# A longer hand-written order at the start of a convolution, Fourier and MLP kernel: the first MLP step's hidden layer and the rest of that step go inside it, and W2 is converted ahead of the third step's statistics

## The chip, the core and the metric

The kernel runs on one core of one Trainium2 chip. The metric is the device time of one execution in microseconds. The engines are TensorE (PE; PEld are its weight loads), VectorE (DVE), ScalarE (ACT), GpSimd (POOL) and SyncE (SP), which issues most of the DMAs.

## What is computed

The reference, cut to what matters. B, S and D are 8, 4224 and 192, the hidden layer has 768 columns.

```python
def _attn_ref(x, weight):                      # 8 heads of 24 columns, 7 taps
    w = softmax(weight)                        # written out with exp and sums
    x_pad = concatenate([zeros((B, 6, D)), x], axis=1)
    ...
    return einsum('hk,bskhg->bshg', w, x_unf)  # a causal convolution over the sequence

def _moe_ref(x, w_ch1, w_ch2):
    mixed = real(fft(fft(x, axis=1), axis=2))
    u = x + mixed
    un = (u - mean(u)) / sqrt(var(u) + 1e-06)  # over the 192 columns
    return u + maximum(un @ w_ch1, 0.0) @ w_ch2
```

The MLP's input is the convolution's output.

## The kernel before

The work is cut into 8 batches (`first` is batch 0, `second` is batch 1) and each batch into 9 steps of the MLP (512 tokens each in steps 0 to 7, 128 in the last). Tile names end in batch and step: `hh_0_1` belongs to step 1 of batch 0. The profile leaves these numbers out.

A batch runs through these stages:

- Convolution, six chunks (`conv_unit`, three parts each): TensorE multiplies windows `xt` with a band matrix into `pc`, ACT copies that to `xa`, DMA stores it to a scratch tensor `sc` in DRAM. ACT also squares `xt` (`sq`), for a scale per batch (`scales`: a norm matmul `pn_x`, a root, `s_x`).
- Split: DMA loads `xs` from `sc` in four pieces (`load_x`), ACT writes the scaled high half in 16 bits to `XH`, DVE the remainder to `XL` (`split_x`, two halves for each piece).
- Fourier stages: `stage_a` (16 tiles, `pa` to `yh` on ACT and `yl` on DVE), `stage_b` (8 tiles, `pb` to `V` on ACT and its low part on DVE, then a small POOL copy to `V0`), and a last product `pq` in `prep`.
- Preparation of a step (`prep`): `pq` to `u` (ACT and POOL; for steps 0 and 1 of batch 0, called `early`, on DVE), the residual rows `xr`, fetched by POOL with four indirect DMAs a step (`load_res`), the statistics (`st`, `mv` on DVE, a root `sd` on ACT, small POOL operations up to `nm`), the normalised `un`, its 16-bit high part `hl` (ACT) and the remainder of `hl` (a subtraction on POOL), then a DMA transpose `kt` on SP (`transposes`).
- MLP of a step: `mlp_hidden`, six groups of five matmuls `ph` (1 group for 128 hidden columns), each read by ACT (`hh`) and DVE (`hlo`); `mlp_out`, 72 matmuls `po` with `W2` and a DVE addition to `u`, then the store.

W1 and W2 come as float64 and are converted on DVE with integer operations (`from_float64`, ten of them for each piece, `cv` and `raw` in the names), scaled by a power of two from their norm (`square_w`, `pow2_of_norm`) and split into high and low parts.

Each engine takes its instructions in one order. Up to the end of the start (all of batch 0's front part, convolution of batch 1, the preparation of steps 0 and 1, the W2 scale) that order is the order in which the code is written: the class `InOrder` puts each instruction behind the last of its engine. Behind `nc.release()` a scheduler orders all that follows. The loop over 72 steps begins there, with `n` = 0: for each it lists the MLP's units and spreads over them the preparation of the steps ahead and the front of the later batches. PSUM tiles named `f` (four buffers) hold `pc`, `pa`, `pb`, `pq` and `pn_x` in turn, those named `h` (two) hold `ph`, those named `o` (two) `po`.

## Time and profile before

| | |
|---|---|
| median of 3 runs | 1275.69 us (1275.05 to 1276.0) |
| the profiled execution, own time | 1266.83 us |
| its span | 1265.0 us |
| mean granted TensorE clock | 0.973 |
| busy in the span: PE, PEld | 1177.6 us (93%), 937.0 us (74%) |
| busy: DVE, ACT, POOL | 753.8 us (60%), 825.7 us (65%), 658.1 us (52%) |

The profiled execution is one execution with the profiler on. Its times run from the first instruction, and sums are made against its span. TensorE is busy for 93% of the span as a mean over the program; the start is different from the rest, so the stretches have to be read apart. In rows of single instructions the columns are the start and the duration in us, engine, line, operation and tiles; what stands in brackets is the idle time of the engine ahead of it and what ended it. The line is 137 for nearly all, since `InOrder` issues them.

### The profile page before, as it was taken

Reading aid. Unit: us, or ns where it says so; the run is one execution under the profiler, and the core shown is the slowest. Engines: PE = TensorE matmul, PEld = TensorE weight load, DVE = VectorE, ACT = ScalarE, POOL = GpSimd, SP = SyncE. Lnnn points to the kernel's source line nnn. Section 1 sums busy time; section 2 is a strip of 40 time slices with the busy share of each in tenths; the row PEclk is TensorE's granted clock in tenths of the full one; section 3 lists DMA queues with packets and bytes.
Section 4 is the critical chain, followed back from the end, with each engine's and each line's share of the span. In section 5 each row is a group of like instructions: output and inputs, shape, how many; then the busy total and the mean of one; then the engine's idle time right before and its main releaser. Section 6 shows DMA issues by size and latency. Waiting matters only on the chain.

```text
span 1265.0 us, 30104 instructions
## 1 busy us (share of the span) xinstructions
PE 1177.6 (93%) x12224; PEld 937.0 (74%) x12224; DVE 753.8 (60%) x1638; ACT 825.7 (65%) x1575; POOL 658.1 (52%) x1036
## 2 busy tenths in 40 slices
PE   4087889999999999998999999999999989999999
PEld 4086668786877878786877878787777867777767
DVE  5685575466556665655665666565755756455444
ACT  4476786587667876568666886577665765555642
POOL 0136553457455655556545673566645575557420
PEclk9597999999999999999999999999999999999999
DMA  8956694686425853386534774358462433224321
GB/s 287 260 128 154 155 230 128 161 196 169 114 70 158 215 136 93 101 187 174 145 95 130 188 175 109 84 148 190 109 135 77 110 91 72 76 64 85 75 60 45
DMA packets 225899, 170.19 MB, mean 135 GB/s; under 512 B 119576, under 2 KB 207456, under 8 KB 225760
## 3 DMA queue, kind: packets, MB, share of 16 engines
q1 hardware_dynamic: 175160, 117.86, 38.9%
q0 software_dynamic: 12672, 25.97, 7.1%
q10 hardware_dynamic: 37928, 24.44, 7.1%
q8 instruction: 95, 1.56, 0.5%
q14 instruction: 44, 0.36, 0.1%
HBM read 83.73 MB, written 58.55 MB: 112 GB/s over the span
## 4 chain that ended last, share of the span: by engine, by line
PE 68%; DMA 7%; DVE 7%; POOL 7%; ACT 5%; issue 4%; SPq 0%; ACTq 0%; DVEq 0%; POOLq 0%
PE ph L137 27%; PE po L137 23%; PE pa L137 6%; PE pq L137 4%; PE pc L137 4%; PE pb L137 4%; POOL xr L137 4%; DVE XL L137 3%; DMA kt<-hl 3%; DMA xs<-sc 2%; ACT un L137 1%; ACT XH L137 1%; POOL u L137 1%; ACT hh L137 1%; POOL hl L137 1%
## 5 line engine op out<-in xcount | busy, mean ns | idle before, releaser
L137 PE MATMUL ph<-kt,W 128*128 128x512 f16 (+1 forms) x2160 | 498.1, 364 | 11.7 <-DMA kt<-hl 6.6
L137 DVE SCALAR_TENSOR_TENSOR hlo<-ph,hh 128x512 f16<-128x512 f32 (+1 forms) x400 | 271.9, 681 | 332.7 <-ACT hh L137 331.8
L137 PE MATMUL po<-W,hh 128*128 128x192 f16 x3168 | 428.7, 247 | 11.4 <-ACT hh L137 8.7
L137 ACT ACTIVATE hh<-ph 128x512 f16<-128x512 f32 (+1 forms) x400 | 237.0, 593 | 303.4 <-PE ph L137 294.2
L137 PE MATMUL po<-W,hlo 128*128 128x192 f16 x1584 | 388.7, 247 | 0.6 <-DVE hlo L137 0.6
L137 POOL DMA_INDIRECT xr<-sc,rows_sb x264 | 291.3, 1103 | 133.7 <-issue 59.9
L137 PEld LDWEIGHTS <-hh 128*128 128x128 f16 x3168 | 282.9, 98 | 45.1 <-ACT hh L137 10.5
L137 PEld LDWEIGHTS <-W 128*128 128x128 f16 x2160 | 193.9, 98 | 153.5 <-issue 17.6
L137 POOL TENSOR_TENSOR u<-u,xr 128x768 f32<-128x768 f32 (+1 forms) x70 | 119.1, 1702 | 123.1 <-ACT u L137 122.9
L137 POOL TENSOR_TENSOR hl<-un,hl 128x512 f16<-128x512 f32 (+1 forms) x144 | 128.4, 914 | 90.7 <-ACT hl L137 90.1
L137 PEld LDWEIGHTS <-hlo 128*128 128x128 f16 x1584 | 155.5, 98 | 16.5 <-DVE hlo L137 0.9
L137 ACT ACTIVATE un<-u,nm,y 128x192 f32<-128x192 f32 x256 | 120.0, 541 | 18.4 <-POOL nm L137 18.4
L137 PE MATMUL pc<-xt,band 128*120 128x144 f32 x756 | 114.1, 295 | 17.9 <-DMA band<-line_d 13.2
L137 PE MATMUL pa<-c_sb,XH 128*128 128x128 f16 x1024 | 104.2, 221 | 23.9 <-ACT XH L137 23.9
L137 PEld LDWEIGHTS pc<-xt,band 128*120 128x120 f32 x756 | 105.1, 190 | 27.1 <-issue 13.2
L137 DVE SCALAR_TENSOR_TENSOR yl<-pa,yh 99x512 f16<-99x512 f32 x128 | 86.6, 688 | 60.7 <-ACT yh L137 60.0
L137 DVE SCALAR_TENSOR_TENSOR XL<-xs,s_x,XH 128x768 f16<-128x768 f32 x64 | 111.0, 1741 | 15.2 <-ACT XH L137 15.0
L137 ACT ACTIVATE XH<-xs,s_x 128x768 f16<-128x768 f32 x64 | 106.2, 1677 | 10.7 <-DMA xs<-sc 10.7
L137 PEld LDWEIGHTS <-XH 128*128 128x128 f16 x1024 | 82.6, 98 | 35.2 <-ACT XH L137 24.0
L137 DVE SCALAR_TENSOR_TENSOR u<-po,fo,u 128x384 f32<-128x384 f32 (+1 forms) x136 | 80.9, 595 | 43.7 <-PE po L137 42.5
L137 PE MATMUL pb<-c_sb,yh 99*128 99x102 f16 (+1 forms) x1040 | 93.4, 210 | 7.3 <-DVE V L137 5.9
L137 PE MATMUL pq<-c_sb,V 128*128 128x130 f16 (+1 forms) x1440 | 99.2, 218 | 0.0
(126 smaller groups left out, 1264.6 us busy)
## 6 DMA issues: line engine op xcount, KB each, us to landing
out_dram<-u SPq DMA_DIRECT2D x64, 384.0 KB, 2.6
xt<-in_xw_dram SPq DMA_DIRECT2D x42, 576.0 KB, 5.2
xs<-sc SPq DMA_DIRECT2D x96, 192.0 KB, 4.0
sc<-xa ACTq DMA_DIRECT2D x30, 540.0 KB, 6.1
xs<-sc SPq DMA_DIRECT2D x32, 216.0 KB, 3.8
sc<-xa SPq DMA_DIRECT2D x12, 540.0 KB, 5.7
xr<-sc,rows_sb POOLq DMA_INDIRECT x264
xt<-in_xv_dram SPq DMA_DIRECT2D x6, 504.0 KB, 4.7
```

What stands on the lines that cost most here:

```text
L137: made = op(*a, **k)
```

## The change

`InOrder` and `Engines` are gone. All instructions built so far are chained, engine by engine, by one call of `keep_order` at the end of the hand-written part, and the loop begins with `n` = 1. What the loop did for step 0 is now written out by hand, in another order:

- The six hidden units of step 0 (`hid[0]` to `hid[5]`) stand among the convolutions of batch 1 and the conversion of W2, ahead of W2's scale.
- W2's scale, its split and the output scale stand ahead of the statistics of step 2 (`stats`).
- The subtraction for `hl` in steps 0 and 1 goes from POOL to DVE.
- The gathers of the residual rows for steps 2 and 3 are issued earlier.
- Chunks 4 and 5 of batch 1's convolution, and its scale, come later; the loads `xs_1_0` and `xs_1_1` come behind the transpose of step 2. Chunk 4's windows take a buffer of `xs` instead of `hh`.
- The rest of step 2's preparation, `u` of step 3 and `stage_b` up to tile 6 are in the written part too.

```diff
+def keep_order(tc):
+    info = mybir.DependencyInfo(
+        mybir.DependencyClass.NoSync, mybir.DependencyReason.DATA
+    )
+    last = {}
+    for ins in tc.nc.cur_bb.bb.instructions:
+        if ins.engine in last:
+            tc.add_manual_dep(ins, last[ins.engine], info, reason="keep_order")
+        last[ins.engine] = ins.name
...
-            nc.gpsimd.tensor_tensor(
+            engine = nc.vector if early else nc.gpsimd
+            engine.tensor_tensor(
                 bl[:, :, o : o + n], un[:, :ng, f], hi[:, :, f], op=ALU.subtract
...
-                load_windows(second, ch, *(("hlo", 2), ("hh", 2), ("hh", 2))[ch - 3])
+                load_windows(second, ch, *(("hlo", 2), ("xs", 2), ("hh", 2))[ch - 3])
...
+    hid = [call(mlp_hidden, first, 0, hts) for hts in hidden_units(0)]
     stage_b(first, 0)
     stage_b(first, 1)
+    for f in gathers(2):
+        f()
     prep_piece(0)
...
     for part in range(2):
         conv_unit(second, 3, part)
     prep_piece(1)
-    for f in gathers(3):
-        f()
+    hid[0]()
     conv_unit(second, 3, 2)
     transposes(first, 1)
     some(half, 2)
+    hid[1]()
     stage_b(first, 2)
-    chunk(second, 4)
     some(half, 2)
+    hid[2]()
+    some(half, 2)
+    hid[3]()
+    some(half, 3)
     total, *stats = sums(2)
     total()
-    some(half, 2)
-    chunk(second, 5)
-    stage_b(first, 3)
-    some(half, 3)
+    hid[4]()
     square_w("w2", mlp["w2_1"], 1)
-    for f in stats:
-        f()
-    stage_b(first, 4)
-    mlp["s2"] = last(pow2_of_norm(mlp["nw2"], 2, 15, "w2"))
+    norm = pow2_of_norm(mlp["nw2"], 2, 15, "w2")
+    next(norm)
+    hid[5]()
+    next(norm)
+    chunk(second, 4)
+    mlp["s2"] = last(norm)
     for i in range(2):
         split2(i)
     output_scale()
-    nc.release()
-    for n in range(len(steps) + 1):
+    for f in stats:
+        f()
+    stage_b(first, 3)
+    for f in gathers(4):
+        f()
+    scale, normal, parts = rest(2)
+    scale()
+    chunk(second, 5)
+    normal()
+    stage_b(first, 4)
+    parts()
+    transposes(first, 2)
+    total, *stats = sums(3)
+    total()
+    last(scales(second))
+    for i in range(2):
+        load_x(second, i)
+        load_windows(batches[2], i)
+    stage_b(first, 5)
+    for f in stats:
+        f()
+    stage_b(first, 6)
+    keep_order(tc)
+    for n in range(1, len(steps) + 1):
```

`keep_order` only fixes the sequence among the instructions of the written part. The scheduler may still put instructions of the loop between them, and does. Below, numbers behind batch and step only tell the tiles of the program apart.

On DVE, around the end of W2's conversion (`raw_w2_1`), before; the statistics of step 2 (`st_0_2`) are the next work, and W2's scale follows behind `V` of tiles 4 and 5:

```order
L137 TENSOR_TENSOR cv0_w2_1_857<-cv0_w2_1_857,raw_w2_1_351 128x576
L137 TENSOR_SCALAR cv1_w2_1_858<-raw_w2_1_351 128x576
L137 SCALAR_TENSOR_TENSOR raw_w2_1_351<-cv1_w2_1_858,cv0_w2_1_857 128x576
L137 BN_STATS st_0_2_1041<-u_0_2_960 128x6
L137 BN_AGGR mv_0_2_1042<-st_0_2_1041 128x2
L137 BN_STATS st_0_2_1041<-u_0_2_960 128x6
L137 BN_AGGR mv_0_2_1042<-st_0_2_1041 128x2
```

And now:

```order
L271 SCALAR_TENSOR_TENSOR raw_w2_1_351<-cv1_w2_1_863,cv0_w2_1_862 128x576
L770 SCALAR_TENSOR_TENSOR hlo_0_0_897<-ph_0_0_4_1004,hh_0_0_896 128x512
L220 TENSOR_REDUCE tot_w2_1014<-nrm_w2_359 128x1
L770 SCALAR_TENSOR_TENSOR hlo_0_0_897<-ph_0_0_5_1018,hh_0_0_896 128x512
L226 TENSOR_SCALAR r_w2_1026<-pn_w2_1016 128x1
L229 RECIPROCAL r_w2_1026<-r_w2_1026 128x1
L231 TENSOR_SCALAR s_w2_1048<-r_w2_1026 128x1
L234 TENSOR_SCALAR s_w2_1048<-s_w2_1048 128x1
L357 SCALAR_TENSOR_TENSOR W2_77<-w2f_265,s_w2_1048,W2_77 128x3x192
L357 SCALAR_TENSOR_TENSOR W2_77<-raw_w2_1_351,s_w2_1048,W2_77 128x3x192
L365 TENSOR_TENSOR fo_78<-s_w1_335,s_w2_1048 128x1
L366 RECIPROCAL fo_78<-fo_78 128x1
```

The scale `s_w2`, both low parts of `W2` and the output scale `fo` now come directly behind the conversion, with the last two `hlo` of step 0 between; `st_0_2` is the next row.

On POOL, the subtractions for `hl` and the gathers `xr` ahead of step 2's `u`, before:

```order
L137 TENSOR_TENSOR hl_0_0_801<-un_0_0_785,hl_0_0_801 128x4x128
L137 TENSOR_TENSOR hl_0_0_801<-un_0_0_785,hl_0_0_801 128x4x64
L137 DMA xr_0_2_805<-sc_0_147,rows_sb_83 128x192 x4
L137 TENSOR_TENSOR hl_0_1_887<-un_0_1_871,hl_0_1_887 128x4x128
L137 TENSOR_TENSOR hl_0_1_887<-un_0_1_871,hl_0_1_887 128x4x64
L137 DMA xr_0_3_891<-sc_0_147,rows_sb_83 128x192 x4
L137 DMA xr_0_4_1164<-sc_0_147,rows_sb_83 128x192 x4
L137 COPY V0_0_658<-V_0_2_907 128x12x8
L137 TENSOR_TENSOR u_0_2_960<-u_0_2_960,xr_0_2_805 128x768
```

And now, the rows from step 2's `u` up to `nm_0_2`, which `un_0_2` on ACT needs:

```order
L659 TENSOR_TENSOR u_0_2_981<-u_0_2_981,xr_0_2_692 128x768
L580 COPY V0_0_658<-V_0_3_1067 128x12x8
L593 DMA xr_0_4_1099<-sc_0_147,rows_sb_83 128x192 x4
L689 TENSOR_SCALAR w_0_2_1107<-mv_0_2_1058 128x4
L690 TENSOR_SCALAR nm_0_2_1108<-mv_0_2_1058 128x4
L692 TENSOR_TENSOR t_0_2_1106<-y_0_2_1105 128x4
L593 DMA xr_0_5_1381<-sc_0_147,rows_sb_83 128x192 x4
L693 TENSOR_TENSOR t_0_2_1106<-t_0_2_1106,w_0_2_1107 128x4
L694 TENSOR_SCALAR t_0_2_1106<-t_0_2_1106 128x4
L695 TENSOR_TENSOR y_0_2_1105<-y_0_2_1105,t_0_2_1106 128x4
L696 TENSOR_TENSOR nm_0_2_1108<-nm_0_2_1108,y_0_2_1105 128x4
```

The subtractions of steps 0 and 1 have left POOL. The gathers `xr_0_2` and `xr_0_3` stand further up, behind `V0` of tiles 0 and 1; `xr_0_4` now stands behind the copy of `V_0_3`, and `xr_0_5` (from the loop) between the operations that lead to `nm_0_2`.

On SP, the transposes `kt` and the loads `xs` of batch 1, before:

```order
L137 DMA xs_1_0_1266<-sc_1_715 32x9x192 x2
L137 DMA_TRANSPOSE kt_0_2_1283<-hl_0_2_1279 128x12x128
L137 DMA xs_1_1_1285<-sc_1_715 32x8x192 x4
L137 DMA xt_2_0_1300<-in_xw_dram 128x1152
L137 DMA xt_2_1_1304<-in_xw_dram 128x1152
L137 DMA xs_1_2_1383<-sc_1_715 32x8x192 x4
L137 DMA out_1_dram<-u_0_0_693 128x768
L137 DMA_TRANSPOSE kt_0_3_1544<-hl_0_3_1489 128x12x128
L137 DMA xs_1_3_1420<-sc_1_715 32x8x192 x4
```

And now:

```order
L804 DMA out_1_dram<-u_0_0_698 128x768
L732 DMA_TRANSPOSE kt_0_2_1178<-hl_0_2_1174 128x12x128
L501 DMA xs_1_0_1218<-sc_1_720 32x9x192 x4
L375 DMA xt_2_0_1223<-in_xw_dram 128x1152
L501 DMA xs_1_1_1225<-sc_1_720 32x8x192 x4
L375 DMA xt_2_1_1230<-in_xw_dram 128x1152
L804 DMA out_1_dram<-u_0_1_742 128x768
L501 DMA xs_1_2_1383<-sc_1_720 32x8x192 x4
L501 DMA xs_1_3_1420<-sc_1_720 32x8x192 x4
L732 DMA_TRANSPOSE kt_0_3_1544<-hl_0_3_1489 128x12x128
```

`xs_1_0` has moved behind `kt_0_2`, and `kt_0_3` behind `xs_1_3`.

More of the change, by code (lines that the diff above doesn't have):

```diff
@@ L122, in token_rows @@
     return rows
-class InOrder:
-    def __init__(self, tc, engine):
-        self.tc, self.engine, self.last, self.fixed = tc, engine, None, True
-    def __getattr__(self, name):
-        op = getattr(self.engine, name)
-        def issue(*a, **k):
-            behind = self.fixed and self.last is not None
-            with self.tc.issue_after(self.last) if behind else ExitStack():
-                made = op(*a, **k)
-            if self.fixed:
-                self.last = made.ins
-            return made
-        return issue
-class Engines:
-    def __init__(self, tc):
-        self.names = ("tensor", "vector", "scalar", "gpsimd", "sync")
-        for name in self.names:
-            setattr(self, name, InOrder(tc, getattr(tc.nc, name)))
-    def release(self):
-        for name in self.names:
-            getattr(self, name).fixed = False
+def keep_order(tc):
[7 more added lines that the diff above has]
+        last[ins.engine] = ins.name
 @with_exitstack
@@ L170 @@
 ):
-    nc = Engines(tc)
+    nc = tc.nc
     PSUM = bass.MemoryType.PSUM
@@ L862, in plan @@
         if b == 1:
-            loads = {-9: [0, 1], -8: [2, 3]}
+            loads = {-8: [2, 3]}
             splits = {-8: [0, 1], -7: [2, 3, 4, 5], -6: [6, 7]}
-            return {}, -9, loads, splits, first_a
+            return {}, None, loads, splits, first_a
         if b == 2:
@@ L883, in front @@
                 units.append(call(load_windows, bt, ch + 2))
-        if bt.b == 2 and rel == min(conv) - 1:
-            units += [call(load_windows, bt, ch) for ch in range(2)]
         if bt.b > 2 and rel in (min(conv) - 2, min(conv) - 1):
@@ L1033 @@
     prep_piece(0)
-    for f in gathers(2):
-        f()
     conv_unit(second, 1, 2)
@@ L1039 @@
     low1(2)
+    for f in gathers(3):
+        f()
     for _ in range(3):
```

2 lines of the change are left out of this document (1 added, 1 removed).

## The prediction

> **What bounds the kernel now.** I read the page first, then busy time by stretch, then TensorE's own instructions in order of time. In the windows the columns are PE, PEld, DVE, ACT and POOL busy us, the granted clock, the DMA share and GB/s.
>
> ```profile
> span 1265.0 us, 30104 instructions
> 85.50:112.70 27.20, 16.57 (x167) 15.46 (x167) 18.54 (x51) 18.32 (x39) 20.76 (x21) 0.80 0.90 217
> 112.70:180.40 67.70, 60.02 (x497) 43.66 (x496) 41.49 (x84) 51.29 (x91) 35.20 (x55) 0.93 0.71 173
> 131.50:174.80 43.30, 37.30 (x305) 27.76 (x304) 24.36 (x43) 35.60 (x57) 19.60 (x34) 0.96 0.88 210
> 180.40:300.00 119.60, 118.93 (x1297) 97.10 (x1298) 71.54 (x154) 86.70 (x165) 64.31 (x104) 1.00 0.68 164
> 300.00:1265.00 965.00, 944.30 (x9843) 744.43 (x9841) 564.94 (x1225) 622.66 (x1209) 528.57 (x845) 0.99 0.47 118
> ...
> 112.74 0.33 PE L137 MATMUL pb<-c_sb,yh 99*128 99x102 f16 x2 [5.42 <-DVE V L137]
> 115.15 2.29 PE L137 MATMUL ph<-kt,W 128*128 128x512 f16 x5
> 121.23 1.24 PE L137 MATMUL ph<-kt,W 128*128 128x512 f16 x5
> 180.42 0.23 PE L137 MATMUL pa<-c_sb,XL 128*128 128x128 f16 x1 [1.67 <-DVE XL L137]
> ```
>
> From 180.40 on TensorE is the bound: idle 0.7 of 119.6 us, then 20.7 of 965. Ahead of that it idles 10.6 us in the first stretch and 7.7 in the second. The changed rows all lie ahead of about 200 us; behind that the two orders are equal on every engine. So I look for one moment: the first `pa` matmul that reads batch 1's `XL` (180.42, after a wait of 1.67 us for DVE). The two orders put the same matmuls ahead of it, but for two of 128x128. If it comes d us later, all that follows should come d later. The question is when the last split of batch 1 ends, and whether TensorE is through with its own work by then.
>
> TensorE will be. The change puts eight `ph` groups (six of step 0, two of step 1) ahead of the first `po`, 1.24 us each, which before stood behind it; the `pb` groups of tiles 4 to 6 move the other way. Were TensorE alone the bound, most of the 18.3 idle us could go: a limit near 1262 us. But ACT and DVE must still feed the split of batch 1.
>
> **Step 1: the subtractions on DVE.**
>
> ```profile
> 85.60 0.84 ACT L137 ACTIVATE hl<-un 128x768 f16<-128x768 f32 x1 [1.46 <-DVE un L137]
> 86.53 2.50 POOL L137 TENSOR_TENSOR hl<-un,hl 128x512 f16<-128x512 f32 x2 [7.28 <-ACT hl L137]
> 86.62 1.88 DVE L137 SCALAR_TENSOR_TENSOR W<-w1a,s_w,W 128x768 f16<-128x768 f32 x1
> 95.55 1.85 POOL L137 TENSOR_TENSOR hl<-un,hl 128x512 f16<-128x512 f32 x2 [1.61 <-ACT hl L137]
> 107.57 0.76 DVE L137 SCALAR_TENSOR_TENSOR raw_w<-cv_w,cv_w 128x576 f32<-128x576 uint32 x1
> L137 DVE SCALAR_TENSOR_TENSOR hlo<-ph,hh 128x512 f16<-128x512 f32 x22 | 14.9, 683 | 20.0 <-ACT hh L137 19.9
> ```
>
> The subtraction of 768 columns has no DVE row. From the 0.76 us that a conversion takes for 576 columns with two inputs it is 1.0; the upper end is POOL's own 2.50. I take 1.0, the row of the same engine. DVE now stands still for ACT's cast (0.84 us from 85.60) and then works 1.0. Against that, `W1`'s low part took 1.88 beside POOL's subtraction; by the `hlo` row (0.68 for 512 columns) it should be 1.0 alone. Together the next step's preparation is 1.0 late on DVE, and its subtraction (1.0 in place of 1.85) ends at 97.4, as before. The first step's transpose can go 1.5 us earlier (87.5 for 89.03). POOL's gathers for steps 2 and 3 move ahead to where POOL waited 7.28 us for the cast, and cost nothing.
>
> **Step 2: W2 to the scale.** From 97.4 DVE carries, ahead of the end of the conversion, four `hlo`, two `V` and nine conversion operations.
>
> ```profile
> L137 DVE SCALAR_TENSOR_TENSOR V<-pb,V 128x408 f16<-128x408 f32 x16 | 8.8, 576 | 7.9 <-ACT V L137 7.8
> 108.42 0.72 ACT L137 ACTIVATE sq_w<-raw_w 128x576 bf16<-128x576 f32 x1 [2.63 <-DVE raw_w L137]
> 115.33 0.16 DVE L137 TENSOR_SCALAR r_w<-pn_w 128x1 f32<-128x1 f32 x1 [0.18 <-PE pn_w L137]
> 116.58 0.78 ACT L137 ACTIVATE W<-w2f,s_w 128x576 f16<-128x576 f32 x1 [0.86 <-DVE s_w L137]
> 119.52 0.15 DVE L137 RECIPROCAL fo<-fo 128x1 f32<-128x1 f32 x1
> ```
>
> Four times 0.6, two times 0.5 and about 5.6 for nine of up to 0.76 give 9.0: the conversion ends at 106.4 instead of 108.3. Then squares 0.8, norm matmul 0.8, the last `ph` of step 0, which now stands between norm and scale, 2.1 (TensorE has idled some 3.7 us for the squares, so I take the 2.29 row and not 1.24), its `hh` and `hlo` 1.1, and the scale 1.2 (115.33 to 116.58): 112.4. ACT has chunk 4's copies and a square (2.4) ahead of W2's high part; W2's two parts and `fo` take 2.5. `fo` is done at 117.3, before at 119.67: 2.4 us gained.
>
> **Step 3: the third step's statistics, POOL's queue.**
>
> ```profile
> 125.71 0.95 POOL L137 DMA_INDIRECT xr<-sc,rows_sb  x1 [0.30 <-issue]
> 131.33 0.19 POOL L137 TENSOR_TENSOR nm<-nm,y 128x4 f32<-128x4 f32 x1
> 131.55 1.87 ACT L137 ACTIVATE un<-u,nm,y 128x192 f32<-128x192 f32 x4 [0.50 <-POOL nm L137]
> L137 DVE BATCH_NORM_STATS2 st<-u 128x6 f32<-128x192 f32 x24 | 7.6, 339 | 1.9 <-POOL u L137 1.9
> ```
>
> Statistics (four, 0.34 and about 0.14 each) and `V_0_3`'s low part end at 120.2. POOL's copy of `V_0_3` waits for that, and now four gathers of 1.25 (0.95 and 0.30 of issue) stand behind that copy, then three small ones, four more gathers, then the rest: 0.3 + 5.0 + 0.8 + 5.0 + 1.1. `nm_0_2` is ready at 132.4; before 131.5. The 2.4 us are gone, on POOL.
>
> **Step 4: ACT up to the last split.** Group rows are for 76 to 182 us: busy in all, mean ns.
>
> ```profile
> L137 ACT ACTIVATE hh<-ph 128x512 f16<-128x512 f32 x22 | 13.1, 596 | 7.5 <-PE ph L137 7.4
> L137 ACT ACTIVATE xa<-pc 120x432 f32<-120x432 f32 (+1 forms) x27 | 12.3, 497 | 2.1 <-PE pc L137 1.4 <-DMA sc<-xa 0.7
> L137 ACT ACTIVATE sq<-xt 128x1152 bf16<-128x1152 f32 x10 | 11.8, 1176 | 0.0
> L137 ACT ACTIVATE V<-pb 128x408 f16<-128x408 f32 x16 | 7.6, 509 | 5.5 <-PE pb L137 5.3
> L137 ACT ACTIVATE u<-pq,g 128x384 f32<-128x384 f32 (+2 forms) x15 | 6.0, 495 | 0.4 <-PE pq L137 0.4
> 140.06 1.45 SPq L137 DMA_TRANSPOSE kt<-hl  x1
> 141.61 2.33 SPq L137 DMA_DIRECT2D xs<-sc  x4
> 145.65 1.78 POOL L137 TENSOR_TENSOR hl<-un,hl 128x512 f16<-128x512 f32 x2 [3.19 <-ACT hl L137]
> 148.52 1.61 ACT L137 ACTIVATE XH<-xs,s_x 128x768 f16<-128x768 f32 x1 [0.71 <-DMA xs<-sc]
> 173.15 1.62 ACT L137 ACTIVATE XH<-xs,s_x 128x768 f16<-128x768 f32 x1
> ```
>
> From `un_0_2` (131.55) to the last `XH` of batch 1 (174.77) ACT was busy 35.6 us and idle 7.7. The new order has in the same stretch also eight `V` (3.8) and two residual moves (2.4), and no longer four `hh` (2.4), a square (1.2) and three `xa` (1.4): 36.8. It begins at 132.4. The wait: `xs_1_0` is now loaded behind `kt_0_2`'s transpose on SP; before, it was loaded ahead of it. The transpose needs `un`, `V_0_4`, an `hh`, the cast and POOL's subtraction (1.8 + 0.9 + 0.5 + 0.8 + 1.8): 138.2, which is 1.9 earlier than before. The loads begin 1.55 later, issue for 2.33 and land 4.6 after that (143.94 to 148.52, where `XH` waited for them): 146.7. ACT's work ahead of `XH` is over at 141.2 (8.8 us after 132.4). So 5.5 us idle, and the last `XH` ends at 132.4 + 36.8 + 5.5 = 174.7. Even.
>
> **Step 5: the last `XL`.**
>
> ```profile
> 175.88 4.48 DVE L137 SCALAR_TENSOR_TENSOR XL<-xs,s_x,XH 128x768 f16<-128x768 f32 x2
> 176.42 2.65 POOL L137 TENSOR_TENSOR u<-u,xr 128x768 f32<-128x768 f32 x1 [1.53 <-ACT u L137]
> 161.28 3.43 DVE L137 SCALAR_TENSOR_TENSOR XL<-xs,s_x,XH 128x768 f16<-128x768 f32 x2
> ```
>
> On DVE `hlo_0_3_1` still stands ahead of the last two `XL`, but its `hh` now comes behind chunk 2's square: `XL` starts 1.1 later, at 177.0. The pair takes 3.43 or 4.48; POOL's addition that ran beside the slower one now follows three copies later, so it meets only the second: I take 3.9, end 180.9 against 180.36. That is d = +0.5.
> The Trainium skill (SBUF — State Buffer, "Who interferes with whom") says that a DVE operation with two inputs in SBUF and a POOL operation that reads SBUF exclude each other, and that the one issued first blocks the other. By that rule both `XL` would be through undisturbed and d near 0.0; by the 4.48 row it would be +1.1. The trace shows a slowing (4.48 for 3.43), not a full block of the pair by 2.65.
>
> **The sum.** -2.4 at `fo`, +3.3 up to `nm_0_2` on POOL, -1.0 up to the last `XH`, +1.2 up to the start of the last `XL`, -0.6 for their length: d is +0.5. The profiled execution took 1266.83 us, 1.83 more than its span; the median shown is 1275.69, 8.9 more. I carry that over: span 1265.5, median 1276.2.
>
> **Rivals.**
>
> ```profile
> DMA to landing us min/median/max: 3.7/3.9/9.2
> ```
>
> Faster: ACT's 5.5 us do not stay idle. If `xs_1_0` lands as `V_0_7` is cast, 4.7 to 5.5 us go, since the 36.8 of work bind alone: d = -4.7, 1271.0. For it speaks that TensorE is eight groups ahead; against it that the wait is on a chain of POOL, SP and DMA, which TensorE's lead does not shorten. It decides from 2.6 us of gain, that is `nm_0_2` ahead of 130.
>
> Slower: `kt_0_3`. It stands on SP behind `xs_1_3` now, and the cast for it ends 11.8 us of ACT work (two `hh`, two squares, `u`, `un`, three `xa`, two `XH`, itself) behind the first `XH` pair (146.7 and 3.4): cast 161.9, subtraction 163.7. At the usual 3.9 it lands at 167.6, its `ph` ends 168.7; `hh_0_3_0` is due on ACT at 171.2, the last `XH` pair less than 3.5 us behind it. At 9.2, the longest in the trace, the `ph` ends at 174.0 and all behind it is 2.8 late: 1279.0, and with the 7.7 us of idle that ACT had before in place of 5.5 it is 1281.2. It decides from a landing over 6.4 us. DMA was busy 0.88 of that stretch, which speaks for it.
>
> **How the numbers follow.** 0.2% of the time, 2.55 us, is about what a measurement tells from no change. My own case, d between -2.5 and +2.5, has 0.42; the faster rival 0.26; the slower 0.32, since a walk along one chain leaves out waits rather than adds them. The range reaches to both rivals, 1271.0 to 1281.5; outside lie the TensorE limit and a case with both waits and a late W2, 0.2 together.
>
> **What would show it.** Right: `fo` near 117, `nm_0_2` near 132, the first `XH` of batch 1 near 147 after a wait for DMA, the first `pa` from `XL` within 2.5 us of 180.4. Wrong: `nm_0_2` ahead of 130 or ACT without an idle stretch ahead of `XH` (faster), or `ph` of step 3 waiting for `kt` (slower). If that `pa` moves and the end does not move with it, the claim that the rest only shifts is wrong.

## The result and the profile after

| | before | after |
|---|---|---|
| median of the runs made together (range) | 1275.37 (1274.59 to 1276.0), 4 runs | 1291.38 (1289.85 to 1292.79), 4 runs |
| ratio to before, 95% interval | 1 | 1.0126 (1.0108 to 1.0143) |
| profiled execution, own time and span | 1266.83, 1265.0 | 1289.85, 1288.0 |
| mean granted TensorE clock | 0.973 | 0.974 |

The change costs 16 us. The forecast was 1276.2 with a range up to 1281.5. The head of the page after:

```profile
span 1288.0 us, 30095 instructions
PE 1180.6 (92%) x12224; PEld 934.8 (73%) x12224; DVE 751.6 (58%) x1642; ACT 820.7 (64%) x1575; POOL 652.7 (51%) x1032
```

TensorE has 3 us more to do than before (1177.6), in a span 23 us longer: the loss is idle time. It lies ahead of the first `pa` from `XL`. These are rows of the timeline after, in order of time, with the idle time before an instruction and what ended it in brackets:

```profile
81.37 0.98 POOL L593 DMA_INDIRECT xr<-sc,rows_sb  x1
90.29 0.95 POOL L593 DMA_INDIRECT xr<-sc,rows_sb  x1 [0.30 <-issue]
91.45 0.53 ACT L438 ACTIVATE xa<-pc 120x432 f32<-120x432 f32 x1 [6.46 <-remote]
92.03 1.32 PE L430 MATMUL pc<-xt,band 128*120 128x144 f32 x4 [6.00 <-issue]
94.19 1.03 DVE L722 TENSOR_TENSOR hl<-un,hl 128x512 f16<-128x512 f32 x2 [6.62 <-ACT hl L718]
96.28 1.02 DVE L342 SCALAR_TENSOR_TENSOR W<-w1a,s_w,W 128x768 f16<-128x768 f32 x1
126.98 0.16 DVE L366 RECIPROCAL fo<-fo 128x1 f32<-128x1 f32 x1
130.02 0.26 POOL L580 COPY V<-V 128x96 f16<-128x96 f16 x1 [16.14 <-DVE V L574]
141.83 0.20 POOL L696 TENSOR_TENSOR nm<-nm,y 128x4 f32<-128x4 f32 x1
142.41 0.60 ACT L769 ACTIVATE hh<-ph 128x512 f16<-128x512 f32 x1 [7.32 <-PE ph L765]
151.85 1.47 SPq L732 DMA_TRANSPOSE kt<-hl  x1
162.31 3.55 ACT L517 ACTIVATE XH<-xs,s_x 128x768 f16<-128x768 f32 x2 [1.92 <-DMA xs<-sc]
166.61 1.83 PE L430 MATMUL pc<-xt,band 128*120 128x144 f32 x7 [4.12 <-DMA xt<-in_xw_dram]
167.93 10.12 SPq L501 DMA_DIRECT2D xs<-sc  x8
176.35 0.86 ACT L718 ACTIVATE hl<-un 128x768 f16<-128x768 f32 x1
177.53 1.78 POOL L722 TENSOR_TENSOR hl<-un,hl 128x512 f16<-128x512 f32 x2
179.33 5.92 SPq L732 DMA_TRANSPOSE kt<-hl  x1
191.29 2.31 PE L765 MATMUL ph<-kt,W 128*128 128x512 f16 x5 [5.05 <-DMA kt<-hl]
199.74 3.04 DVE L521 SCALAR_TENSOR_TENSOR XL<-xs,s_x,XH 128x768 f16<-128x768 f32 x2
202.83 0.23 PE L539 MATMUL pa<-c_sb,XL 128*128 128x128 f16 x1
```

Two kinds of loss show. First, two stalls while POOL issues eight gathers in one piece. From 84.99 to 91.45 ACT stands for something the profile calls "remote", for which it shows no work of this program, and TensorE waits 6.00 us for nothing that the profile shows; POOL's gathers run from 81.37 to 91.24. Before 142.41 ACT waits 7.32 us for `ph`, and the gathers between POOL's copy and `nm_0_2` run from 130.44 to 140.92. Second, step 3 is late: `kt_0_3` leaves SP at 179.33, where the first trace of before has 148.5. On SP it stands behind `xs_1_2` and `xs_1_3` (167.93 to 178.05), but that is not what holds it: its own input, POOL's subtraction, ends only at 179.31, and the cast ahead of that on ACT begins at 176.35. TensorE then has no `ph` of step 3 to do and waits 5.05 us for it, and earlier 4.12 us for a window `xt`. The first `pa` from `XL` comes at 202.83, before at 180.42: 22.4 later, in a span 23.0 longer.

### The profile page after: what moved, and what is told of

Its sections match the earlier page's. It is cut to its first block, busy times and chain, and to the rows that moved or that the text cites. A ratio compares the mean times of both kernels' runs of the same rounds, so it can differ in the third digit from the quotient of the medians.

```text
span 1288.0 us, 30095 instructions
## 1 busy us (share of the span) xinstructions
PE 1180.6 (92%) x12224; PEld 934.8 (73%) x12224; DVE 751.6 (58%) x1642; ACT 820.7 (64%) x1575; POOL 652.7 (51%) x1032
## 4 chain that ended last, share of the span: by engine, by line
PE 73%; DMA 7%; ACT 5%; DVE 5%; POOL 5%; issue 4%; another core or an unknown queue 1%; SPq 0%; ACTq 0%; POOLq 0%; DVEq 0%
PE ph L765 28%; PE po L790 8%; PE po L784 8%; PE po L787 8%; PE pa L539 6%; PE pc L430 5%; PE pq L623 5%; PE pb L565 4%; DMA kt<-hl 4%; POOL xr L593 2%; DVE XL L521 1%; ACT un L707 1%; DMA sc<-xa 1%; DMA xs<-sc 1%; ACT hh L769 1%
## 5 line engine op out<-in xcount | busy, mean ns | idle before, releaser
L765 PE MATMUL ph<-kt,W 128*128 128x512 f16 (+1 forms) x2160 | 497.4, 364 | 19.5 <-DMA kt<-hl 12.2
L784 PE MATMUL po<-W,hh 128*128 128x192 f16 x1584 | 387.8, 246 | 12.0 <-ACT hh L769 10.3
L787 PE MATMUL po<-W,hh 128*128 128x192 f16 x1584 | 387.3, 246 | 0.5 <-issue 0.2
L765 PEld LDWEIGHTS <-W 128*128 128x128 f16 x2160 | 194.0, 98 | 163.7 <-issue 17.3
L784 PEld LDWEIGHTS <-hh 128*128 128x128 f16 x1584 | 155.1, 98 | 30.7 <-ACT hh L769 12.4
L722 POOL TENSOR_TENSOR hl<-un,hl 128x256 f16<-128x256 f32 (+2 forms) x140 | 122.9, 899 | 100.9 <-ACT hl L718 95.7
L787 PEld LDWEIGHTS <-hh 128*128 128x128 f16 x1584 | 154.8, 98 | 16.9 <-issue 2.0
L430 PEld LDWEIGHTS pc<-xt,band 128*120 128x120 f32 x756 | 107.8, 194 | 34.0 <-issue 20.8
L521 DVE SCALAR_TENSOR_TENSOR XL<-xs,s_x,XH 128x768 f16<-128x768 f32 x64 | 108.2, 1697 | 15.5 <-ACT XH L517 13.3
```

What stands on the lines that cost most here:

```text
L430: nc.tensor.matmul(pc[:WR, h - h0], band[:, h, :WR], xt[:, :, h * GRP : (h + 1) * GRP], start=True, stop=True,)
L521: nc.vector.scalar_tensor_tensor(part(XL), src, bt.c, part(XH), op0=ALU.mult, op1=ALU.subtract)
L722: engine.tensor_tensor(bl[:, :, o : o + n], un[:, :ng, f], hi[:, :, f], op=ALU.subtract)
L765: nc.tensor.matmul(ph[:, n], W1[:, w, ht * 128 : (ht + 1) * 128], kt[:, k], start=(i == 0), stop=(i == len(order) - 1),)
L784: nc.tensor.matmul(po[:, g % 2], hh[:, ht, tk], W2[:, ht, 0], start=(ht == 0), stop=False)
L787: nc.tensor.matmul(po[:, g % 2], hh[:, ht, tk], W2[:, ht, 1], start=False, stop=False)
```

## The experiments

Kernels run together shared one chip and the runs of before. The level of before differed from one such group to another on the same chip (1259 to 1274 us), so times are compared inside a group: by the ratio, which stands with its 95% interval behind each time, and, where microseconds are given, by the difference of the medians. Where two kernels differ by one edit, the diff is that edit.

**The base.** The profiled execution of before (1266.83) had been 8.9 us shorter than its median.

> The kernel before, unchanged, for a second trace of it. Its first trace has a span of 1265.0 us and no idle time without a releaser on TensorE or ACT; its other runs took 1275.0 to 1276.0. If the difference of 8.9 us is a matter of the execution, this trace should have a span near 1273.5 and show, somewhere ahead of 200 us, about 8 us of idle time that the first lacks. If the first trace is typical, the span is 1265 to 1267 again and the new stalls in the changed kernel (ACT 6.46 us until 91.45, TensorE 6.00 until 92.03) belong to the change.

1274.44, span 1272.7: a profiled execution near the median. Its last `XL` ends at 186.2, not 180.4. It also has what the first trace lacks, waits of TensorE that no semaphore explains (from 60 to 112 us: total, number, longest):

```profile
PE pb L137 <- issue: 6.6, 8, 2.4
```

The longest of the eight ends at 96.45, beside four gathers of POOL; the other seven lie from 106.9 to 112.0, beside and just behind eight gathers that POOL issues in one piece (100.49 to 110.33). The first trace has eight in one piece too, from 97.55 on, and no such wait. So stalls of this kind are not new with the change. After's first `pa` from `XL` is therefore 16.6 later than in a comparable trace of before, and its median is 16.0 longer. What follows is measured against this trace. Its windows over the stretch of the changed order (columns as in the prediction: PE, PEld, DVE, ACT and POOL busy, clock, DMA share, GB/s):

```profile
85.00:112.00 27.00, 17.66 (x160) 15.64 (x159) 16.60 (x49) 17.01 (x36) 17.57 (x18) 0.90 0.95 218
112.00:140.00 28.00, 25.07 (x223) 18.45 (x224) 18.90 (x55) 16.78 (x36) 17.56 (x26) 0.79 0.28 74
140.00:180.00 40.00, 33.58 (x272) 24.89 (x270) 22.67 (x40) 31.52 (x51) 16.36 (x29) 0.96 0.95 218
180.00:215.00 35.00, 33.24 (x383) 27.69 (x382) 24.42 (x44) 24.88 (x50) 18.70 (x24) 1.00 0.52 132
```

And the same windows after:

```profile
85.00:112.00 27.00, 16.40 (x108) 11.65 (x106) 18.31 (x54) 13.33 (x27) 5.58 (x6) 0.81 0.72 163
112.00:140.00 28.00, 20.72 (x190) 17.04 (x190) 12.07 (x29) 10.69 (x23) 9.51 (x13) 0.88 0.22 59
140.00:180.00 40.00, 31.66 (x286) 23.67 (x285) 21.85 (x48) 27.80 (x51) 21.20 (x33) 0.96 0.70 161
180.00:215.00 35.00, 25.35 (x230) 19.06 (x231) 19.40 (x39) 25.09 (x45) 16.74 (x25) 0.85 0.80 200
```

From 85 to 215 TensorE idles 35.9 us after (130 less the four PE sums) and 20.5 before: 15.4 more, against 16.0 us of time.

Three theories were then open. *Stalls*: the gathers in one piece, which the change moves ahead, hold ACT and TensorE up. *The split*: batch 1's `xs` and scale come late, and so its last `XL`. *Step 3*: its sum and its `kt` come late, and TensorE runs dry.

**The gathers in one piece: held back, and early in the kernel before.** The first kernel is after with a 16-column POOL copy that reads the last columns of DVE's subtraction, and the gathers of steps 2 and 3 behind it, about where before has them. The second is before with these gathers moved up.

```diff
+    def gate(it):
+        seen = sb.tile([128, 16], F16, tag="seen", name=f"seen_{it}", bufs=2)
+        nc.gpsimd.tensor_copy(seen, first.hl[it][:, 10, 112:128])
...
-    for f in gathers(2):        # and gathers(3), likewise
-        f()
     ...
     transposes(first, 0)
+    gate(0)
+    for f in gathers(2):
+        f()
```

> The changed kernel with the eight gathers for steps 2 and 3 held back: on POOL a 16-column copy that reads the DVE subtraction of step 0 stands ahead of the four for step 2, and one of step 1 ahead of the four for step 3. Theory 1 (the subtraction that left POOL lets eight gathers issue in one piece at 81.4 to 91.2, and ACT stands still until they are through): ACT's stall of 6.46 us at 85 goes, the first transpose issues near 89 in place of 95.5, and the time falls by 5 to 8 us, to 1283 to 1286. Theory 2 (the loss lies later: the gathers for step 4 ahead of the third step's mean on POOL, and the loads of batch 1 behind two transposes on SP): within 2.5 us of 1291.4. Theory 3 (the stalls come with the execution and not with the order): the stall stays or moves, time within 2.5 us of 1291.4.

1287.81, ratio 1.0112 (1.0074 to 1.015). The first stall is gone: `xa` at 83.95 waits 0.18, `kt_0_0` goes at 88.1 instead of 95.5. The second is there (6.98 before the `hh` at 136.78). The last `XL` ends 8 us earlier than after's (194.4), but the time is still 15.8 us over before's, where after's is 16.0 to 18.2 over it (here and below).

```diff
     stage_b(first, 1)
+    for f in gathers(2):
+        f()
     ...
-    for f in gathers(2):
-        f()
     ...
     low1(2)
+    for f in gathers(3):
+        f()
     ...
-    for f in gathers(3):
-        f()
```

> The kernel before with one part of the change alone: the gathers for steps 2 and 3 are issued where the change puts them (behind the second tile's copy of V0), so that all eight run at 79 to 89 us; POOL keeps the subtractions. Theory 1 (eight gathers in one piece hold up ACT): ACT's first copy of chunk 1 waits several us, step 0's subtraction on POOL is later too, and the time grows by 4 to 8 us, to 1279 to 1284. Theories 2 and 3: within 2.5 us of 1275.4.

1271.11, 0.9998 (0.9975 to 1.0021). Early gathers alone cost nothing that shows where the rest of the order is before's. The edit did not bring the piece of the changed kernel, though: the subtraction on POOL (88.15) divides the gathers, four from 80.63 on and eight from 90.66 on. Beside the eight ACT stands 4.31 us for "remote", up to 102.28, and the time is that of before all the same.

**The split's loads and scale first.** After with the scale and the first two loads of batch 1 ahead of step 2's transposes; in the first of the two, step 4's gathers also go behind `parts()`.

```diff
-    for f in gathers(4):        # not moved in the second kernel
-        f()
     ...
     normal()
     stage_b(first, 4)
+    last(scales(second))
+    for i in range(2):
+        load_x(second, i)
     parts()
+    for f in gathers(4):        # not in the second kernel
+        f()
     transposes(first, 2)
     ...
-    last(scales(second))
     for i in range(2):
-        load_x(second, i)
         load_windows(batches[2], i)
```

> The changed kernel with two moves behind 120 us: batch 1's scale and its first two loads stand ahead of the third step's last part and its transpose, and the gathers for step 4 stand behind that part on POOL, so the mean's small operations no longer wait for them. Up to 115 us nothing differs. Theory 2: the first XH of batch 1 starts near 152 in place of 162.3 and the last XL ends some 8 to 10 us earlier, time 1281 to 1284. Theory 1: what is lost at 85 to 92 stays, and the rest is a shift: a gain of at most 3 us, 1288 to 1291. In both the trace tells whether the stall at 85 to 91 comes again in a kernel that is the same up to there.

1284.22, 1.0078 (1.0046 to 1.0109). The first `XH` begins at 141.5 instead of 162.3, step 2's transpose goes at 140.8 instead of 151.8, and yet `kt_0_3` still goes at 180.8 and the last `XL` ends at 196.7. The start of the split was 21 us earlier, its end 6.

> The changed kernel with one move: batch 1's scale and its first two loads stand ahead of the third step's last part and its transpose; the gathers for step 4 stay where the change put them, ahead of the third step's mean. Theory 2 (the loads behind the transpose on SP cost the most of it): the first XH starts near 143 in place of 162, step 3's mean is no later than 161, its transpose issues near 170 and not behind the loads of pieces 2 and 3; last XL near 192, time 9 to 11 us under the changed kernel. Rival: XH's early start only pushes step 3's normalisation and transpose back on ACT and SP, as in the kernel with both moves, where it had its mean at 175.3 and its transpose at 180.8: last XL 196 to 200, time 3 to 6 us under the changed kernel.

1288.93, 1.0102 (1.0072 to 1.0132). The first `XH` begins at 152.6, the last `XL` ends at 200.3. `kt_0_3` goes at 182.8.

**After once more, the subtractions back on POOL, and both edits.**

> The changed kernel, unchanged, for a second trace and for a time beside the others on one chip. If its stall on ACT at 85 to 91 belongs to the order, it is there again (it was 6.46 us in the first trace and 4.91 in the kernel that is the same up to 115 us); the last XL of batch 1 should end near 202 and the ratio to the kernel before lie inside 1.011 to 1.014. If the stall comes with the execution, it is gone or elsewhere and the last XL ends near 196.

1292.57, 1.0147 (1.0087 to 1.0207), with the same stalls: 6.45 before `xa` at 91.54, 7.33 before `hh` at 142.95.

```diff
-            engine = nc.vector if early else nc.gpsimd
+            engine = nc.gpsimd
```

with `gathers(2)` and `gathers(3)` at their places of before:

> The changed kernel with its first part undone: both early subtractions back on POOL and the gathers for steps 2 and 3 at the places they had before; all from the second step's hidden units on stays changed. If the first part (DVE subtraction and early gathers) costs what the held-back gathers saved (last XL 202.8 to 194.4), this has the last XL near 195 to 198 and a time 5 to 7 us under the changed kernel's. If the DVE subtraction by itself is a gain of about 1.5 us at the first transpose, as predicted, this is some 1 to 2 us slower than the kernel with held-back gathers. If the first part is of no weight, it is within 2.5 us of the changed kernel.

1287.37, 1.01 (1.0071 to 1.0129). No first stall (`xa` at 85.15 waits 0.18); `hh` at 139.72 waits 9.31. The subtractions and their gathers are not what costs the most.

The gate and the loads first together:

> The changed kernel with both repairs: the gathers for steps 2 and 3 held back by a small copy on POOL behind each DVE subtraction, and batch 1's scale and first two loads ahead of the third step's last part. If the two losses are separate (8.4 us at the last XL from the gathers, 6 or more from the loads), they add: last XL at 186 to 189, time within 2.5 us of the kernel before. If step 3's chain is what sets the end in both, the second repair adds less than 3 us to the first: last XL 192 to 195 and a ratio to the kernel before of 1.006 to 1.009.

1290.29, 1.0111 (1.0065 to 1.0158), `kt_0_3` at 181.3. The two edits do not add up to a repair.

**Gathers replaced by plain loads.** In after and in before, the 16 indirect gathers of steps 2 to 5 of batch 0 become plain loads of the same size; the residuals of these four steps are then other rows.

```diff
+        if b == 0 and 2 <= it <= 5:
+            r0 = 128 * (4 * (it - 2) + g)
+            nc.gpsimd.dma_start(bt.xr[it][:, g], bt.sc[r0 : r0 + 128])
+            return
```

> The changed kernel; the sixteen indirect gathers of steps 2 to 5 of batch 0 are replaced by plain loads of 128 consecutive rows at the same places of POOL's queue (so the residuals of these four steps are of other rows; sizes, queue and order are the same). If issuing indirect gathers in one piece is what holds ACT and TensorE, both stalls go (6.5 and 0.9 us at 85 to 93, 7.2 at 135 to 142): last XL near 202 - 14 = 188 and a time 10 to 15 us under the changed kernel, near the kernel before. If it is the traffic of the loads, or only their place in the queue, the stalls stay and the time is within 3 us of the changed kernel.

1271.7, 1.0092 (1.0068 to 1.0115), in a group whose before is 1259.15. Neither stall is there. Rows of its timeline, and under them its waits of TensorE from 112 to 215 (total us, number, longest):

```profile
122.02 2.17 POOL L594 DMA_DIRECT2D xr<-sc  x4
129.47 0.60 ACT L773 ACTIVATE hh<-ph 128x512 f16<-128x512 f32 x1 [2.59 <-PE ph L769]
...
PE pc L430 <- DMA xt<-in_xw_dram: 6.3, 1, 6.3
PE po L788 <- ACT hh L773: 5.3, 3, 3.1
PE ph L769 <- DMA kt<-hl: 5.0, 1, 5.0
```

> The kernel before with the same replacement for steps 2 to 5 (other rows in the residuals of these four steps). Its gathers for steps 2 to 5 ran beside less dense TensorE work, and its second trace lost 5.8 us at the last XL against its first, with idle time on TensorE between 92 and 112 us. If that is the gathers too, this trace looks like the first one (last XL near 180, span 1265 or less) and the median falls by 5 to 9 us. If the first trace was a chance of another kind, the median is within 2.5 us of the kernel before.

1261.19, 1.0011 (0.9988 to 1.0033). Against it, after with the same edit is 10.5 us slower (1271.7 less 1261.19), without a stall and with cheap loads. Most of the loss is not the gathers. The waits above say where it stays: `xt` and `kt` are waited for as in after. That the plain loads took the stalls away is not shown: after with its own gathers was not run in this group, and the next kernel, in the same group, issues eight gathers in one piece (from 95.92 on) without a stall.

Before with the gate of the first experiment and one more edit:

```diff
-            nc.gpsimd.tensor_tensor(
+            engine = nc.vector if early else nc.gpsimd
+            engine.tensor_tensor(
```

> The kernel before with one part of the change alone: both early subtractions on DVE, the gathers for steps 2 and 3 held at their old places in time by a 16-column copy on POOL behind each subtraction. Predicted for this part: the first transpose 1.5 us earlier, the second as before, nothing at the end: within 2.5 us of the kernel before. Rival: the DVE stands still for ACT's cast, W1's low part and the second step's statistics come later, and the time grows by 1 to 3 us.

1260.74, 1.0006 (0.9989 to 1.0023). The subtractions on DVE alone cost and gain nothing that shows.

**The split's last tiles earlier, on another chip.** `plan` places the split of batch 1's halves 6 and 7 one step earlier, first in after.

```diff
-            splits = {-8: [0, 1], -7: [2, 3, 4, 5], -6: [6, 7]}
+            splits = {-8: [0, 1], -7: [2, 3, 4, 5, 6, 7]}
```

> The changed kernel with the last pair of batch 1's XH and XL one step earlier in the plan, so that on ACT it stands ahead of step 3's first hh and no longer behind its wait for step 3's transpose. If that wait sets the end: XH of the last pair starts at 184 to 187 in place of 194, the first pa from XL reads at 190 to 194 in place of 202.8, and the time falls by 8 to 11 us (ratio to the kernel before about 1.005). If TensorE or the loads set it, the pair may come earlier, but the end moves by less than 3 us (ratio 1.011 to 1.014).

1272.14, 1.0089 (1.0054 to 1.0124), before being 1259.88. The eight gathers are in one piece (80.1 to 90.1), but `xa` at 84.33 waits 0.18 and `hh` at 132.99 only 2.59: the same piece of POOL work with no stall. `kt_0_3` goes at 170.6, the first `pa` from `XL` at 185.9.

The same with the gate:

> The same with the gathers for steps 2 and 3 held back behind the DVE subtractions. If both losses are what they look like, they add: first pa from XL at 183 to 187, ratio to the kernel before 0.998 to 1.003. If the end does not follow the last XL, ratio 1.008 to 1.012.

1269.5, 1.0081 (1.005 to 1.0113). Where the first stall does not occur, holding the gathers back is worth nothing that shows.

Before with the same `plan`:

> The kernel before with the same earlier place for the last pair. There the hh ahead of it waits 0.75 us only, so if that wait is what the changed kernel lost, little is to be had here: 0 to 4 us (the pair passes two hh, a square and three copies of 0.5 to 1.2 us), ratio 0.997 to 1.000. If an earlier last XL always moves the end by as much, the ratio is 0.995 to 0.997.

1259.1, 0.9994 (0.9967 to 1.002). Its timeline:

```profile
165.18 3.09 DVE L137 SCALAR_TENSOR_TENSOR XL<-xs,s_x,XH 128x768 f16<-128x768 f32 x2 [2.32 <-ACT XH L137]
168.33 0.23 PE L137 MATMUL pa<-c_sb,XL 128*128 128x128 f16 x1 [0.61 <-DVE XL L137]
```

The moment that the prediction watched comes 12 us earlier (168.3 for 180.4), and the time is the same. From that `pa` to the end it is now 1092.8 us (1261.1 less 168.3), in the first trace of before 1084.6: the rest took 8.2 us longer. Of the 12, some 2.6 are not the edit's: `kt_0_3`, which it does not move, goes at 145.9 here and at 148.5 there. A trace of before itself from this chip was not taken.

After with this `plan`, the gate, the scale and loads first and step 4's gathers behind `parts()`:

> The changed kernel with gathers for steps 2 and 3 held back, gathers for step 4 behind the third step's last part, batch 1's first two loads ahead of that part, and the last XH pair one step earlier. The last XL no longer waits for step 3 at all: first pa from XL at 172 to 178. If the end follows, ratio 0.991 to 0.997, faster than both; if TensorE then waits for step 3's transpose instead (180 to 185 in the kernels with the loads first), the gain is eaten and the ratio is 1.000 to 1.006.

1270.63, 1.0097 (1.0064 to 1.0131). The last `XL` pair ends as early as in the kernel just shown:

```profile
164.25 3.09 DVE L521 SCALAR_TENSOR_TENSOR XL<-xs,s_x,XH 128x768 f16<-128x768 f32 x2 [1.02 <-ACT XH L517]
...
177.01 1.45 SPq L732 DMA_TRANSPOSE kt<-hl  x1
```

`kt_0_3` goes at 177.01, almost as late as in after, TensorE waits 5.34 us for it, and the first `pa` from `XL` begins only at 186.94, 19.6 us behind the end of the last `XL`. The split is done some 11 to 14 us earlier than in the two versions above with the early split (181.0 and 178.6), and the loss stays. That sets the split theory aside, and leaves step 3.

**Step 3's chain.** After again, then after with step 3's sum ahead of step 2's normalisation, as the loop had it in before:

> The changed kernel, unchanged, a third time. If the stalls of ACT (6.5 us at 85) and TensorE (at 135 to 142) belong to the order, both are there again, whatever the kernel before takes in this group. If they belong to the group of runs, they come together with a kernel before of 1272 to 1275 and not with one near 1260; without them the last XL ends near 191 to 193 and the ratio to the kernel before is 1.008 to 1.011, with them 1.012 to 1.015.

1291.22, 1.0162 (1.0129 to 1.0195), stalls of 6.35 and 7.16.

```diff
     scale, normal, parts = rest(2)
     scale()
+    total, *stats = sums(3)
+    total()
     chunk(second, 5)
     normal()
+    for f in stats:
+        f()
     stage_b(first, 4)
     parts()
     transposes(first, 2)
-    total, *stats = sums(3)
-    total()
     last(scales(second))
     ...
-    for f in stats:
-        f()
```

> The changed kernel with step 3's residual sum and statistics written right behind the third step's scale, where they no longer wait for its transpose; its normalisation and transpose follow in the loop, and on SP its transpose then stands ahead of the loads of pieces 2 and 3. If TensorE's want of step 3's transpose (5 us of waiting for it, and about as much for hh behind it) is what is left, the transpose issues 12 to 20 us earlier, near 155 to 160, the waits for it go, and the time falls by 5 to 9 us: ratio 1.002 to 1.006. If the last XL sets the end, it moves by what XL moves, 2 us or less.

1284.33, 1.0116 (1.0077 to 1.0155): 6.9 us of the 18.0 are back (by the ratios 5.9 of 20.6). The two intervals overlap; five of its six runs lie below all six of after. The last `XL` ends 3.8 us earlier (198.9 for 202.7). `kt_0_3` goes at 159.1, and the wait for it is gone; more waits for `xt` stand in its place:

```profile
PE pc L430 <- DMA xt<-in_xw_dram: 8.6, 2, 5.7
PE pn_w L223 <- DVE tot_w L220: 4.5, 1, 4.5
PE po L784 <- ACT hh L769: 3.5, 3, 2.6
```

So batch 2's windows go ahead of that place, and step 3's normalisation and transposes into the written order; the early split is in as well.

```diff
     total()
     chunk(second, 5)
+    for i in range(2):
+        load_windows(batches[2], i)
     normal()
     ...
     last(scales(second))
+    scale, normal, parts = rest(3)
+    scale()
     for i in range(2):
         load_x(second, i)
-        load_windows(batches[2], i)
     stage_b(first, 5)
+    normal()
+    parts()
+    transposes(first, 3)
     ...
-        if n + 2 < len(steps):
+        if n > 1 and n + 2 < len(steps):
```

> The changed kernel with step 3's sum, statistics, normalisation and transpose all in the written order, batch 2's first two loads ahead of batch 1's on SP, and the last XH pair one step earlier. If the waits for step 3's transpose (5 us), for hh (3 to 6) and for batch 2's first load (4 to 6) are the 10 us that are left, all of them go: ratio 0.993 to 1.001 without the stalls, some 0.003 more with them. If something else holds TensorE back between 140 and 180, ratio 1.005 or more.

1277.53, 1.0056 (1.0035 to 1.0077): 13.7 of the 18.0 us are back (by the ratios 13.5 of 20.6). Its waits and its last two windows:

```profile
PE po L784 <- ACT hh L769: 5.1, 2, 2.6
PE pn_w L223 <- DVE tot_w L220: 4.7, 1, 4.7
PE ph L765 <- DVE hlo L770: 4.1, 3, 2.4
...
140.00:180.00 40.00, 32.64 (x302) 24.56 (x300) 24.88 (x53) 32.69 (x57) 22.63 (x31) 0.94 0.93 236
180.00:215.00 35.00, 34.23 (x390) 27.77 (x390) 21.99 (x44) 27.15 (x55) 21.50 (x34) 1.00 0.65 155
```

TensorE no longer waits for `kt` or `xt`; from 180 to 215 it idles 0.8 us, after 9.7. With 4.3 us left (7.1 by the ratio) it is still slower than before, although its first `pa` from `XL` begins at 185.15, ahead of that in the second trace of before (186.24). Four edits are in it at once, the early split among them, so what each of them is worth is not shown, beyond the sum of step 3 in the kernel ahead of it. The first stall is still in this kernel (4.95 and 1.60 us). This kernel with its gathers held back was not run, so that the stall is the remainder is not shown. No version of the changed kernel beat the kernel before.

**The measure that goes with the time.** TensorE's idle time from 85 to 215, from the windows, and what the time did:

| kernel | idle | more idle than | more time in its group |
|---|---|---|---|
| after | 35.9 | before, 20.5: +15.4 | +16.0 |
| after, step 3's sum first | 32.7 | +12.2 | +11.1 |
| after, step 3 and loads first | 24.2 | +3.7 | +4.3 |
| after, plain loads | 28.1 | before with plain loads, 18.3: +9.8 | +10.5 |
| before, early split | 18.2 | 18.3 in the first trace: -0.1 | -0.8 |
| after, gathers held back | 29.1 | +8.6 | +15.8 |
| after, early split | 26.1 | before, early split, 18.2: +7.9 | +13.0 |

Five of these seven agree within 1.1 us, the last two fall short by 5 and 7. The other eight traces of the changed kernel and its versions fall short as well, by 2.6 to 7.3 us: after itself in its two repeats has 13.5 and 14.3 more idle for 18.2 and 18.0 more time. By the ratios, two of the five agree less well: 14.8 and 7.1 us of time for 12.2 and 3.7 of idle. And one trace of the same kernel differs from another by 2.2 (18.3 and 20.5 in before). The measure tells the direction each time, and most of the size for the changed kernel, but it is not the whole account. Busy time holds no record of how fast the work went (the granted clock was 0.85 from 180 to 215 after, 1.00 in before), which may be part of the rest; that was not tried by itself.

## Why the prediction was wrong, and where it was right

**The step that failed: step 4, ACT up to the last split.** These are the five terms of the prediction's sum, read at the same five points in after and in the second trace of before. Each is what is added behind the one above it:

| term, up to | foretold | measured |
|---|---|---|
| `fo` (step 2) | -2.4 | +2.2 |
| `nm_0_2` on POOL (step 3) | +3.3 | +3.3 |
| the end of the last `XH` (step 4) | -1.0 | +11.3 |
| the start of the last `XL` (step 5) | +1.2 | +1.2 |
| the end of the last `XL` (step 5) | -0.6 | -1.4 |
| d | +0.5 | +16.6 |

Step 4 is off by 12.3 us, step 2 by 4.6 (the first stall, 6.5, lies ahead of `fo`), the rest by less than 1. (Against the first trace of before, with which the sum was made, d is 22.4; the base, below, has 5.8 of it.) Step 4 took ACT's work and one wait, 36.8 and 5.5 us, and called the result even. The work was about right: from `nm_0_2` (142.03) to the end of the last `XH` (197.47) ACT is busy for 38.4. The wait is the term that was mis-sized: ACT is idle for 17.0. Only 1.9 of that is the wait for `xs_1_0`, for which the 5.5 stood. In 8.2 ACT waits for TensorE (`ph`, `pb`, `po`), in 4.1 ahead of the `un` at 188.23, and 2.5 have no releaser. The walk let `un_0_2` begin as soon as `nm_0_2` is ready; three `hh` stand ahead of it on ACT, each waiting for its `ph`, and it begins 4.1 us later (146.10).

**One moment for the whole.** The prediction said that TensorE "will be" through with its own work, so that all that follows shifts with the last `XL`. Both moved together in after (22.4 and 23.0), which looked like a confirmation. The early split in before shows that it is none: the `pa` came some 10 us earlier and the time stayed. After with the early split and the loads first shows it from the other side: its last `XL` ends 11 to 14 us earlier than in the two versions beside it, and the time is not lower. What went with the time better, though not closely, is how much TensorE gets done in the whole stretch. The prediction's test for this claim was the right one, but only an experiment could apply it.

**The slower rival came true, for another reason and at another price.** `ph` of step 3 waited for `kt_0_3`. Its reason, the place behind `xs_1_3` on SP, was not what held `kt_0_3`: SP was free at 178.05, the subtraction ended at 179.31. Its walk from the first `XH` pair to the cast was right (11.8 foretold, 11.4 measured: 165.86 to 177.21), but the first `XH` began 15.6 us late (162.31 for 146.7), and the transpose went as much later (179.33 for 163.7). Then its `ph` began 12.0 us behind it (191.29), more than the 9.2 that the rival allowed at most. The price of 2.8 to 5.0 us counted only what a late `hh_0_3_0` would do to the last `XH` on ACT, and not that TensorE had nothing else to do. The rival also priced `kt` alone, while step 3's sum, written behind step 2's transposes, is late too: the last operation for `nm_0_3` begins at 160.9, in the traces of before at 140.9 and 145.8. Moving the sum up gave 6.9 us; with windows, step 3's parts and the early split as well it was 13.7 in all.

**TensorE's lead was counted as a gain.** The eight `ph` groups ahead of the first `po` were read as work done early, "a limit near 1262". The same move leaves less work for 180 to 215, as long as step 3 is not ready: 25.4 us of PE there, in the second trace of before 33.2.

**The stalls had no term.** That the gathers ahead of DVE's subtraction "cost nothing" failed in after: the `hl` cast and all behind it came 6.5 us late. On the other chip the same piece cost 0.18. In the three groups in which after itself was run (before at 1273 to 1275 us) it is 16.0 to 18.2 us slower; in the two with before at 1259 to 1260 it is 12.3 to 12.6, with plain loads or with the early split, and no trace of these two shows a stall. That puts the stalls at some 3 to 6 us, an estimate across groups and edits, and net of what stalls cost before itself; holding the first one's gathers back gave 0.2 to 2.4.

**The base.** The sum was made against a profiled execution 8.9 us shorter than its median, and these 8.9 were carried over. The second trace of before is 7.7 us longer than the first, and 5.8 of them lie ahead of its last `XL`, in the very stretch that the sum walks through. The 1265.0 trace showed the chain without a stall.

**What was right.** The subtraction takes 1.03 on DVE (1.0 foretold), `W1`'s low part 1.02 without POOL's beside it (1.0). From POOL's copy to `nm_0_2` it takes 12.0 us (130.02 to 142.03; the terms give 12.2). `pn_w` waits 4.8 for the squares (3.7). `kt_0_0` goes 5.4 us behind the start of the `xa` copy ahead of it (83.61 in the first trace of before) in five traces in which POOL subtracts, and 4.1 to 4.3 behind it in the seven in which DVE does and the first stall does not fall: 1.1 to 1.3 earlier, 1.5 foretold. `fo` is 2.3 earlier with plain loads (118.8 for 121.1; 2.4 foretold), though not with the early split (122.3 for 118.1). What was not: from the first `XH` to the end of the last it takes 35.2 after (162.31 to 197.5), not 28.0; the loads of the last two pieces issue only from 167.93 on. The last `XL` pair takes 3.04, not 3.9. POOL's addition starts 0.9 us before its end, leaves it undisturbed, and takes 2.50 itself instead of 1.81. That is what the rule of the Trainium skill (SBUF — State Buffer, "Who interferes with whom") gives, and the prediction was wrong to read the pair of 4.48 as a slowing that speaks against it (rows in the last section); the result hung on neither value.

## What to carry to other kernels

Before walking one chain to one moment, sum the idle time of the bounding engine over the whole stretch, and ask of each of its next inputs when it comes; a moment that moves with the end need not set it. When a queue is walked, add up its waits as well as its work: here the work was right and the waits were three times what was reckoned. When work is moved ahead on the bounding engine, follow the work that was to fill its place: here the preparation of the next step, its sum, its cast and its transpose. Where a transfer stands behind others on a queue, look when its own input was ready before the queue is blamed. And take a second profiled execution of the kernel before where the first lies far off the median.
